# Two moves in a hand-written order: two weight products in front of a batch's scores, and softmax sums one group later

## The chip, the core and the metric

The kernel runs on one NeuronCore of a Trainium2 chip. The metric is the device time of one execution in microseconds (us). The inputs lie in device memory at the start, the output lies there at the end; the host does no arithmetic.

## What is computed

A Linformer attention over 8 batches of 8 heads, 1024 tokens, head size 64, followed by a feed-forward block with an activation close to hard-swish. Cut to what matters:

```python
k_proj = einsum('ks,bhsd->bhkd', E, k)          # 1024 tokens -> 64 rows
v_proj = einsum('ks,bhsd->bhkd', F, v)
attn   = softmax(q @ k_proj.T / 8)              # 1024 x 64 per head
x      = (attn @ v_proj).reshape(8 * 1024, 512)
h      = x @ w_in                               # 512 -> 2048
g      = h * clip(h + 3, 0, 6) / 6
out    = g @ w_out                              # 2048 -> 512
```

## The kernel before, in words

The work of a batch is done in two blocks of 512 tokens (`t` is 0 or 1), and a block has two halves.

The first half makes `g`. It is a row of 16 groups (`fo`, written L0 to L15 in the orders below): `first_group` multiplies 128 columns of `w_in` with the block's `xT` (8 matmuls, helper line L189), ACT takes the activation out of PSUM (L535), DVE multiplies and writes one chunk of `g` in bf16 (L536). PSUM has four buffers of the pool `mm` for this (`pmm`) and four of the pool `at` (`pat`).

The second half multiplies `g` with `w_out`. Except in the first block of all, it is done as seven block products in place of eight: `g` and `w_out` are cut into 2 x 2 blocks, and sums and differences of blocks are multiplied (class `Sums` makes those of `g`, POOL and an early part of the kernel those of `w_out`, in `w_sums`). A `Pair` covers two times 128 tokens; a block has a pair A and a pair B. A name such as A7 is product 7 of pair A: 16 matmuls of 128x256 (L189), in `step`. Which operands a product reads:

- 7: block a22 of `g` as it is, and a sum of weights. 2: a11 as it is, and a difference of weights. Both open a PSUM tile of their own and are copied out (L665); 5 accumulates into the tile of 2 and is copied out.
- 5: `sc` = a11 + a21 (`sums.c`). 6: a21, overwritten by a22 - a21 (`sums.a`). 1: `sb`, a difference of a11 and the new a21 (`sums.b`). 3: `sd` (`sums.d`, two pieces on POOL). 4: a12.
- 6, 1, 3 and 4 accumulate one after another into one tile, `self.x`; between them DVE subtracts what stands in it from a copy (`sub`, L136) and so gets the output rows. The next product may start only when that subtraction has read the tile.

A block's second half is done while the next block's first half runs. The order of all this on TensorE is written out by hand, engines run their own instructions in program order, and a framework adds the waits. Two orders matter here.

Batch 0's second block, lines 706 to 734. Its second half is not woven with groups, but with batch 1's attention, which comes in four visits (V0 to V3, `visit`, L278 for sums and values, L257 for scores). V0 computes the scores of heads in three pairs from `qT` and `kT`, which two transposing DMAs (L177) and one more (L240) have to bring, and the exps of them on ACT (L266): four score tiles in `pat`, two in `pmm`. V1 does the softmax sums of the first pair with a matmul over ones, its values, the scores of the fourth pair, logs (L195), the inverse (L201) and the exps of the fourth. V2 and V3 do the rest; R is the rest of a visit, the DVE products (L290) that write `xT` of batch 1. The four sums of blocks are made behind the steps that `added` names; `pair.copy` says which copies go to ACT (A7, B7, A5), the others go to DVE.

The blocks of batch 1 and later run through `START` (the first block of batch 1) and `ORDER`. Other work is hung on places of these orders by `at((t, place), work)`; `done(place)` runs it behind the place. From batch 2 on, the softmax sums are not matmuls: `add_up(j)` adds one pair's weights on DVE (L298, transposing), `sums_turned` and `spread_sums` (the reciprocal and two kinds of DMA, L319 and L325) bring their inverse back over all rows, and `some_values` multiplies with it. For batch 2 this is hung on batch 1's blocks (lines 767 to 776). `some_scores` gives the first pair's exps at once and lets those of the second be called one by one behind later groups (`pop`).

At the start of a block the first lines do `behind[0].sums.a(KH - 2, KH)` (the last two chunks of a21), then L0, then `sums.b` and `sums.d`, then the places hung on L0.

Of the kernel before, what the change touches and what calls it, by code (L numbers as in the profile page):

```python
# [15 lines left out]
def kernel(  # L16
# [11 lines left out]
    nc = tc.nc  # L28
# [45 lines left out]
    def g_tile():  # L74
        return gpool.tile([P, FO, TOK], bf16, tag="g", name="g")
# [52 lines left out]
    KH, MH = FO // 2, d_model // 2  # L128
# [76 lines left out]
    def behind_that(last, *what):  # L205
        mark = att.tile([1, 1], bf16, tag="mark", name="mark")
        nc.gpsimd.tensor_copy(mark, last)
        load_kqv(*what)
# [3 lines left out]
    class Attention:  # L212
# [38 lines left out]
        def scores(self, j, *allocs):  # L251
            qT = qT_dma[self.b]
            tiles = [alloc() for alloc in allocs]
            for a in range(2):
                for t in range(NB):
                    for r in range(2):
                        nc.tensor.matmul(tiles[r][t * KP:(t + 1) * KP, a * HT:(a + 1) * HT],  # L257
                                         self.kT[r * D:(r + 1) * D, 2 * j + a, :],
                                         qT[r * D:(r + 1) * D, j, a, t * HT:(t + 1) * HT],
                                         start=True, stop=True)  # L260
            return tiles
# [23 lines left out]
        def values(self, j, *allocs):  # L285
            return self.quads(lambda r, h: self.vp[r:r + KP, h, :], j, allocs)
# [7 lines left out]
        def add_up(self, *js):  # L294
            if self.parts is None:
                self.parts = att.tile([P, KO, 32], f32, tag="parts", name="parts", bufs=1)
            for j in js:
                nc.vector.tensor_reduce(out=self.parts[:, j], op=ALU.add, axis=mybir.AxisListType.X, apply_transpose=True,  # L298
                                        in_=self.aT[j].rearrange("p a r n -> p (a r n)").rearrange(
                                            "p (c i) -> p c i", i=32))  # L300
# [237 lines left out]
    def first_group(xT, t, g, fo):  # L538
        h_ps = pmm()
        h_part(h_ps, xT, t, fo, range(KO))  # L540
        h_out(h_ps, g, fo)
# [20 lines left out]
    def x_tile():  # L562
        return xpool.tile([P, KO, NB, TOK], bf16, tag="xT", name="xT")
# [45 lines left out]
    def pop():  # L609
        if later:  # L610
            later.pop(0)()
# [94 lines left out]
    sums = Sums(g[1])  # L706
    behind = [Pair(0, 1, sums, p, beside=pmm) for p in range(2)]
    TwoGroups(xT, 1, g[1]).parts((0, 1), (2, 3))
    for fo in range(2, FO):
# [6 lines left out]
            sub(b21, b21, b22, nc.gpsimd)  # L716
        elif fo == 5:
            second.projected()
    added = {"A7": lambda: sums.c(nc.vector), "A2": lambda: sums.a(0, KH), "A5": sums.b, "V1": sums.d}
    for what in "V0 A7 A2 B7 A5 V1 A6 R B2 A1 V2 B5 R A3 B6 V3 A4 B1 R".split():  # L720
        if what[0] == "V":
            while later:
                pop()
            rest = second.visit(int(what[1:]))
        elif what[0] == "R":
            rest()
        else:
            pair = behind["AB".index(what[0])]
            pair.copy = nc.scalar.copy if what in ("A7", "B7", "A5") else nc.vector.tensor_copy
            pair.step(int(what[1:]))  # L730
            pop()
        if what in added:
            added[what]()
# [10 lines left out]
    for b in range(1, B):  # L744
        if b + 1 < B:
            x_next = second.xT = x_tile()
        third = Attention(b + 2) if b + 2 < B else None

        plan = {}

        def at(place, *what):
            plan.setdefault(place, []).extend(what)

        def scores(*js):
            return lambda: second.some_scores(js)

        def values(*js):
            return lambda: second.some_values(*js)

        def add_up(*js):  # L760
            return lambda: second.add_up(*js)

        def spread(turned, inverted):
            at(turned, lambda: second.sums_turned())
            at(inverted, lambda: second.spread_sums())

        if b == 1:
            at((0, "L0"), second.projected)
            at((0, "L8"), second.load_next)
            at((0, "N5"), scores(0, 1))  # L770
            at((0, "L14"), add_up(0))
            at((0, "L15"), add_up(1))
            at((1, "L1"), scores(2, 3))
            at((1, "L2"), add_up(2))
            at((1, "L3"), add_up(3))
            spread((1, "B2"), (1, "L5"))
        elif b == 2:
            at((0, "L2"), second.projected)
            at((0, "A4"), second.load_next)
            at((0, "A4"), scores(0, 1))  # L780
            at((0, "B6"), scores(2))
            at((0, "L10"), add_up(0))
            at((0, "B1"), scores(3), add_up(1))
            at((0, "B3"), add_up(2))
            at((1, "A6"), add_up(3))
            spread((1, "A1"), (1, "L4"))
            at((1, "L4"), third.projected)
        elif b + 1 < B:
            if b == 3:
                at((0, "L1"), second.load_next)  # L790
            at((0, "L1"), scores(0, 1))
            at((0, "B7"), add_up(0))
            at((0, "A1"), scores(2, 3), add_up(1))
            at((0, "A3"), add_up(2))
            at((0, "A4"), add_up(3))
            spread((0, "B6"), (0, "L10"))
            if third:
                at((0, "B4"), lambda: third.projected(pause=False))
                if third.b + 1 < B:
                    at((1, "L12"), third.load_next)  # L800
        if b < 3:
            at((1, "N2"), values(0))
            at((1, "L12"), values(1))
            at((1, "B3"), values(2))
            at((1, "L14"), values(3))
            if b == 1:
                at((1, "B3"), lambda: behind_that(second.recs[1][:1, 0, :1], 3, "q"))
        elif b + 1 < B:
            at((1, "A1"), values(0, 1))
            at((1, "A4"), values(2, 3))  # L810

        def done(place):
            for f in plan.pop((t, place), ()):
                f()

        for t in range(NB):
            g = g_tile()
            sums = Sums(g)
            start = (b, t) == (1, 0)
            pairs = {"A": behind[0], "B": behind[1], "N": Pair(b, t, sums, 0, (b, t) == (B - 1, NB - 1))}  # L820
            if not start:
                behind[0].sums.a(KH - 2, KH)
            done("start")
            for what in START if start else ORDER:
                n = int(what[1:])
                if what[0] != "L":
                    pairs[what[0]].step(n)
                    done(what)
                    if what == ("N5" if start else "B3"):
                        sums.a(0, KH - 2)  # L830
                    continue
                if b < 4 and t == 0 and n < 2:
                    if n == 0:
                        first_two = TwoGroups(xT, t, g)
                    for fo in range(2):
                        first_two.part(fo, range(n * (KO - 1), KO - 1 + n))
                    if n == 1:
                        first_two.out()
                else:
                    first_group(xT, t, g, n)  # L840
                pop()
                if n == KH - 1:
                    sums.c()
                if not start and n == 0:
                    behind[0].sums.b()
                    behind[0].sums.d()
                done(what)
            behind = [pairs["N"], Pair(b, t, sums, 1, (b, t) == (B - 1, NB - 1))]
        assert not plan, plan
        second, xT = third, x_next  # L850

    sums = behind[0].sums
# [35 lines left out]
```

## Time and profile before

| what | us |
|---|---|
| three runs | 484.77, 486.40, 486.26; median 486.26 |
| the profiled execution | 484.99 |
| its span, first to last instruction | 483.2 |
| TensorE busy | 474.6 (98%) |
| DVE busy | 330.5 (68%) |
| ACT busy | 263.5 (55%) |
| GpSimd busy | 175.5 (36%) |

The profile has PE for TensorE's matmuls, PEld for its weight loads, DVE for VectorE, ACT for ScalarE, POOL for GpSimd and SP for SyncE, which issues DMAs. In the order of time a line has the start in us from the first instruction, the duration, the engine, the source line, what is written <- what is read, the shape, how many instructions are put together, and in brackets the idle time in front with what ended it. In the list of waits: who <- for what, total us, how often, the longest. Matmuls overlap, so a run of them is counted from start to start.

### The profile page before, as it was taken

How to read it: one execution, taken by the hardware profiler on the slowest of the kernel's cores; microseconds unless marked ns; L12 is line 12 of the kernel's file. 1: busy time of each engine (PE TensorE's matmuls, PEld its weight loads, DVE VectorE, ACT ScalarE, POOL GpSimd, SP SyncE). 2: the span in 40 equal slices, each digit the busy share in tenths (PEclk: the TensorE clock that was granted, in tenths of full speed). 3: DMA queues.
4: the chain of work that ended last, by engine and by line, in shares of the span. 5: the costliest groups of instructions: out<-in, count | busy, mean ns of one | idle time of the engine just before them, and what ended most of it. 6: DMA issues, size and time to landing. Idle time of an engine off the chain costs nothing.

```text
span 483.2 us, 14296 instructions
## 1 busy us (share of the span) xinstructions
PE 474.6 (98%) x6210; PEld 330.2 (68%) x6210; DVE 330.5 (68%) x546; ACT 263.5 (55%) x502; POOL 175.5 (36%) x107
## 2 busy tenths in 40 slices
PE   8899989999999999999999999999999999999997
PEld 3554558657676776776777777777777777777777
DVE  2582368678865858886777857777777977756463
ACT  3666588675457553745457454655547444445441
POOL 8634953134335231533423235330333333140420
PEclk9999999999999999999999999999999999999999
DMA  9999999864976979499998295955911081111012
GB/s 164 198 201 207 232 154 214 182 109 94 241 135 114 211 162 231 107 201 206 208 176 161 79 224 107 210 112 121 221 45 46 26 206 60 45 45 45 35 43 101
DMA packets 84590, 68.61 MB, mean 142 GB/s; under 512 B 38320, under 2 KB 70576, under 8 KB 84528
## 3 DMA queue, kind: packets, MB, share of 16 engines
q0 software_dynamic: 33008, 29.36, 39.0%
q1 hardware_dynamic: 51152, 37.83, 32.3%
q8 instruction: 48, 0.79, 0.7%
q10 hardware_dynamic: 368, 0.52, 0.4%
q14 instruction: 14, 0.11, 0.1%
HBM read 71.83 MB, written 16.97 MB: 184 GB/s over the span
## 4 chain that ended last, share of the span: by engine, by line
PE 93%; DMA 4%; POOL 1%; DVE 1%; SPq 0%; issue 0%; ACT 0%; POOLq 0%
PE mm L189 71%; PE at L189 18%; DMA w_in_sb<-in_moe_w_in_dram 2%; PE at L278 2%; PE at L257 2%; DMA qT<-q 1%; DMA k<-in_k_dram 1%; SPq L177 0%; PE at L447 0%; POOL q L103 0%; DVE g L536 0%; ACT r L535 0%; DVE parts L298 0%; POOL k L107 0%; PE at L427 0%
## 5 line engine op out<-in xcount | busy, mean ns | idle before, releaser
L189 PE MATMUL mm<-xT,w_in_sb 128*64 128x512 bf16 x2048 | 254.2, 380 | 0.3 <-DMA w_in_sb<-in_moe_w_in_dram 0.3
L536 DVE SCALAR_TENSOR_TENSOR g<-r,mm 128x512 bf16<-128x512 f32 x256 | 173.9, 683 | 114.4 <-ACT r L535 112.2
L535 ACT ACTIVATE r<-mm 128x512 f32<-128x512 f32 x256 | 152.1, 597 | 147.4 <-PE mm L189 130.5
L189 PEld LDWEIGHTS <-w_in_sb 128*64 128x64 bf16 x2048 | 114.3, 110 | 72.8 <-issue 6.5
L189 PEld LDWEIGHTS <-g 128*64 128x64 bf16 x2048 | 112.3, 110 | 30.4 <-issue 3.2
L136 POOL TENSOR_TENSOR sd<-g,sb 128x1024 bf16<-128x1024 bf16 x28 | 59.0, 2124 | 146.3 <-DVE sb L136 73.7
L133 POOL TENSOR_TENSOR sc<-g 128x2048 bf16<-128x2048 bf16 x14 | 57.0, 4069 | 111.7 <-DVE g L536 111.7
L189 PE MATMUL mm<-w_out_sb,g 128*64 128x256 bf16 (+1 forms) x1088 | 77.2, 286 | 0.0
L189 PE MATMUL at<-w_sums,g 128*64 128x256 bf16 x896 | 58.3, 273 | 0.7 <-DVE g L536 0.7
L665 ACT COPY m<-at 128x256 f32<-128x256 f32 x84 | 31.3, 373 | 24.8 <-PE at L189 24.7
L290 DVE TENSOR_TENSOR xT<-at,rec 128x512 bf16<-128x512 f32 x54 | 36.0, 683 | 1.6 <-DMA rec<-turned_rows 1.0
L189 PE MATMUL mm<-w_out_sb,sd 128*64 128x256 bf16 x480 | 31.1, 273 | 0.0
L189 PE MATMUL mm<-w_sums,sb 128*64 128x256 bf16 x480 | 31.0, 273 | 0.0
L189 PEld LDWEIGHTS <-sd 128*64 128x64 bf16 x480 | 26.7, 110 | 5.3
L189 PEld LDWEIGHTS <-sc 128*64 128x64 bf16 x480 | 26.4, 110 | 5.7 <-issue 0.8
L189 PEld LDWEIGHTS <-sb 128*64 128x64 bf16 x480 | 26.4, 110 | 5.3
L266 ACT ACTIVATE aT<-at 128x512 bf16<-128x512 f32 x52 | 29.2, 596 | 1.1 <-PE at L257 0.6
L298 DVE TRANSPOSE_TENSOR_REDUCE parts<-aT 128x32 f32<-128x1024 bf16 x24 | 29.7, 1237 | 0.0
L189 PE MATMUL at<-w_out_sb,sc 128*64 128x256 bf16 x448 | 29.3, 273 | 0.0
L136 DVE TENSOR_TENSOR o_sb<-m,mm 128x256 f32<-128x256 f32 x60 | 24.8, 413 | 3.6 <-PE mm L189 3.5
L136 DVE TENSOR_TENSOR g<-g 128x1536 bf16<-128x1536 bf16 (+2 forms) x29 | 20.4, 703 | 0.6
L136 DVE TENSOR_TENSOR sb<-g 128x2048 bf16<-128x2048 bf16 x15 | 18.3, 1220 | 0.1
(91 smaller groups left out, 275.6 us busy)
## 6 DMA issues: line engine op xcount, KB each, us to landing
out_dram<-o_sb SPq DMA_DIRECT2D x60, 256.0 KB, 4.1
rec<-turned_rows SPq DMA_DIRECT2D x48, 256.0 KB, 6.4
k<-in_k_dram POOLq DMA_DIRECT2D x7, 1024.0 KB, 10.2
v<-in_v_dram POOLq DMA_DIRECT2D x7, 1024.0 KB, 15.6
q<-in_q_dram POOLq DMA_DIRECT2D x7, 1024.0 KB, 20.6
w_out_sb<-in_moe_w_out_dram POOLq DMA_DIRECT2D x4, 512.0 KB, 14.8
w_in_sb<-in_moe_w_in_dram POOLq DMA_DIRECT2D x7, 256.0 KB, 10.0
k<-in_k_dram POOLq DMA_DIRECT2D x4, 256.0 KB, 5.7
```

The lines of the kernel that those rows point to most:

```text
L133: engine.tensor_tensor(out=out, in0=x, in1=y, op=ALU.add)
L136: engine.tensor_tensor(out=out, in0=x, in1=y, op=ALU.subtract)
L189: nc.tensor.matmul(ps[lo:lo + width], stationary[:, lo:lo + width], moving, **flags)
L257: nc.tensor.matmul(tiles[r][t * KP:(t + 1) * KP, a * HT:(a + 1) * HT], self.kT[r * D:(r + 1) * D, 2 * j + a, :], qT[r * D:(r + 1) * D, j, ...
L266: when(lambda r=r: nc.scalar.activation(aT[:, :, r, :], tiles[r].rearrange("p (a n) -> p a n", a=2), AF.Exp, scale=scale))
L278: nc.tensor.matmul(tiles[t][c:c + D], stationary(r, 2 * j + a), self.weights(j, a)[r:r + KP], start=True, stop=True)
L290: when(lambda t=t: nc.vector.tensor_mul(self.xT[:, j, t, :], av[t], rec[:, t]))
L298: nc.vector.tensor_reduce(out=self.parts[:, j], op=ALU.add, axis=mybir.AxisListType.X, apply_transpose=True, in_=self.aT[j].rearrange("p a ...
L535: nc.scalar.activation(r, h_ps, AF.Relu, bias=0.5, scale=1.0 / 6.0)
L536: nc.vector.scalar_tensor_tensor(g[:, fo, :], r, 1.0, h_ps, op0=ALU.min, op1=ALU.mult)
L665: self.copy(m, ps)
```

## The change

```diff
-    added = {"A7": lambda: sums.c(nc.vector), "A2": lambda: sums.a(0, KH), "A5": sums.b, "V1": sums.d}
-    for what in "V0 A7 A2 B7 A5 V1 A6 R B2 A1 V2 B5 R A3 B6 V3 A4 B1 R".split():
+    added = {"A7": lambda: sums.c(nc.vector), "V0": lambda: sums.a(0, KH), "A5": sums.b, "V1": sums.d}
+    for what in "A2 A7 V0 B7 A5 V1 A6 R B2 A1 V2 B5 R A3 B6 V3 A4 B1 R".split():
...
             at((0, "N5"), scores(0, 1))
-            at((0, "L14"), add_up(0))
-            at((0, "L15"), add_up(1))
+            at((0, "L15"), add_up(0))
+            at((1, "L0"), add_up(1))
             at((1, "L1"), scores(2, 3))
```

In batch 0's second block, products 2 and 7 of pair A are issued before V0, in this order; they stood behind it as 7, 2. So on ACT the copy of A7 stands in front of V0's six exps, on DVE the copy of A2 in front of `sc`, and the in-place difference `sums.a` is issued behind V0. The buffers of the pool `mm` go round otherwise: A2 and A7 take those of groups 12 and 13, the two score tiles of V0 those of 14 and 15, B7 the one that A7's copy frees, and V1's scores the two that V0's exps free.

In batch 1's first block, `add_up(0)` of batch 2 stands on DVE behind the last chunk of `g` (group 15), not in front of it, and `add_up(1)` stands behind group 0's chunk and `sb` of the next block; it stood behind group 15's chunk. The instructions of TensorE and ACT keep their order there. GpSimd's and SP's orders are the same in both kernels.

## The prediction

> **What bounds the kernel now.** I read the page first, then the list of waits, then the order of time around the two places that the diff touches.
>
> ```profile
> PE 474.6 (98%) x6210; PEld 330.2 (68%) x6210; DVE 330.5 (68%) x546; ACT 263.5 (55%) x502; POOL 175.5 (36%) x107
> ...
> PEclk9999999999999999999999999999999999999999
> ```
>
> TensorE is busy for 474.6 of 483.2 us, at full granted clock in every slice. So nothing can come from doing less: the change moves work and removes none. What it can win is TensorE idle time inside 60 to 130 us. The list of waits in that stretch shows what there is to win:
>
> ```profile
> PEld L257 <- DMA qT<-q: 2.0, 1, 2.0
> ...
> PE at L189 <- DVE g L536: 0.7, 1, 0.7
> ```
>
> Two stalls: about 2 us where scores wait for the transposed queries, 0.65 us where a product waits for the last piece of `g`. All else of TensorE's there is issue gaps of 0.2 to 0.4 us. Taken whole, the two would be some 2.5 us, or 0.5%, which is also about what a measurement of this kernel can tell from no change. The question is what is late next.
>
> **Part 1, products 2 and 7 of pair A ahead of V0.** These lines are the order of time around V0:
>
> ```profile
> 58.56 8.80 PE L189 MATMUL mm<-xT,w_in_sb 128*64 128x512 bf16 x80
> ...
> 67.29 0.63 PE L257 MATMUL at<-qT,kT 64*64 64x256 bf16 x16
> ...
> 67.90 2.06 ACT L266 ACTIVATE aT<-at 128x512 bf16<-128x512 f32 x4
> 68.03 0.69 DVE L536 SCALAR_TENSOR_TENSOR g<-r,mm 128x512 bf16<-128x512 f32 x1 [0.18 <-ACT r L535]
> ...
> 69.62 0.41 PE L257 MATMUL mm<-qT,kT 64*64 64x256 bf16 x8 [1.70 <-DMA qT<-q]
> ...
> 69.96 2.81 PE L189 MATMUL mm<-w_sums,g 128*64 128x256 bf16 x48
> ...
> 71.07 0.37 ACT L665 COPY m<-mm 128x256 f32<-128x256 f32 x1
> ...
> 73.69 0.37 ACT L665 COPY m<-mm 128x256 f32<-128x256 f32 x1 [0.50 <-PE mm L189]
> ...
> 74.02 1.08 ACT L195 ACTIVATE rec<-at 128x512 f32<-128x512 f32 x2
> ...
> 75.14 1.06 ACT L201 ACTIVATE rec<-rec 128x1024 f32<-128x1024 f32 x1
> ...
> 76.23 1.29 DVE L290 TENSOR_TENSOR xT<-at,rec 128x512 bf16<-128x512 f32 x2 [0.29 <-ACT rec L201]
> ...
> 77.55 0.51 PE L278 MATMUL at<-aT,ones 64*64 64x512 bf16 x4
> ```
>
> The reader is to see three things. TensorE idles from 67.66 to 69.62 before the eight scores of the third pair of heads. ACT has one exp after another from 67.90. And the sums of 77.55 start just when the DVE products (76.23 + 1.29 = 77.52) let go of their PSUM tiles.
>
> TensorE's side. The 80 matmuls from 58.56 take 0.108 each, so TensorE is free at 67.2. A product is 16 matmuls; the 48 from 69.96 end where the next group begins, at 72.61, so one is 0.87. A2 runs 67.2 to 68.1, A7 to 68.95. A2 reads chunks of `g` that are long written, and its PSUM buffer was freed at 66.1. A7's last two matmuls come at 68.84 and need the chunk that DVE writes from 68.03 to 68.72: no wait. V0's first 16 scores then run from 69.05 to 69.4, and the last eight still wait for the second transpose, which lands at 69.58 whatever TensorE does. So V0 ends at 69.96 as now, but B7 comes next, instead of A7 and A2: TensorE is **1.73 us ahead** here (2 x 0.87).
>
> ACT's side. The copy of A7 now stands in front of the six exps, not behind them. It can start 0.25 after A7, at 69.2, and holds ACT for 0.33 (73.69 to 74.02). The exps, which started at 67.90, start at 69.53. They start 0.49 apart, so ACT gets to the copies of B7 and A5 at 72.45, 0.33 each, and to V1's two logs at 73.12. Now those start at 74.02. So ACT is only **0.90 ahead** of now. Two waits of TensorE take the rest: V1's scores need two PSUM buffers that the last two exps read until 72.57 (TensorE comes at 72.25: 0.35), and V2's sums need the tiles that the DVE products read. These follow the logs: 1.12 to the inverse, 1.06 for it, 1.29 for two products. That was 77.52 and becomes 76.62, so B5 starts at 77.08 and not 77.98.
>
> From 77.54 to 83.84 ACT stands still for nothing (its rows of logs and inverses follow each other), and the chain of logs, inverses and products feeds the next hidden layer; so 0.90 stays, neither more nor less. DVE: A2's copy now comes before `sc`, which ends at 70.20 instead of 69.86, needed by A5 at 70.83. The in-place difference and `sb` come at 70.23 and 71.48 instead of 72.28 and 73.53. sd on GpSimd follows `sb` and ends at 77.0; A3 needs its second half at 78.4. The orders of GpSimd and SP are the same, and loads and transposes of batch 2 are triggered by the same transposes. The k and v of batch 2 land 9.7 and 13.9 us after issue, v at 81.1, and are used at 83.7: cover of 2.6. Its q lands at 86.9; its transposes are due at 88.1: cover of 1.2, and behind that 2 us more until the scores. Value taken: -0.90. Bounds: 0, if the logs start where they do now; -1.73, if neither wait comes.
>
> **Part 2, sums over batch 2's weights one group later.** I keep the present clock; part 1 shifts all of it alike.
>
> ```profile
> 103.88 1.24 DVE L298 TRANSPOSE_TENSOR_REDUCE parts<-aT 128x32 f32<-128x1024 bf16 x1
> ...
> 104.17 0.93 PE L189 MATMUL at<-w_sums,g 128*64 128x256 bf16 x14
> ...
> 105.04 0.65 DVE L536 SCALAR_TENSOR_TENSOR g<-r,mm 128x512 bf16<-128x512 f32 x1
> ...
> 105.75 0.30 PE L189 MATMUL at<-w_sums,g 128*64 128x256 bf16 x2 [0.65 <-DVE g L536]
> ...
> 110.00 0.69 DVE L536 SCALAR_TENSOR_TENSOR g<-r,mm 128x512 bf16<-128x512 f32 x1 [0.19 <-ACT r L535]
> ...
> 117.31 0.35 DVE L136 TENSOR_TENSOR o_sb<-mm,m 128x256 f32<-128x256 f32 x1
> ...
> 117.84 1.04 PE L189 MATMUL mm<-w_out_sb,g 128*64 128x256 bf16 x16
> ```
>
> DVE has the sum of 103.88 in front of the last gated piece of `g` (105.04), and the last two matmuls of A7 wait for this until 105.75. With the sum behind it, the piece starts when ACT gives its input, 104.25, and ends at 104.94, when TensorE arrives at 104.93. TensorE leaves A7 at 105.09, not 105.88: **0.79 ahead**.
>
> But DVE does the same work, and it is what is full: from 103.28 to 117.97 its rows follow each other with one gap, 0.19 at 110.00. I add start to start. Now, 103.28 to 110.00: 6.72. After: gated piece 0.97 (0.37 of it idle until 104.25), piece 0.60, sum 1.16, in-place difference 0.30, piece 0.60, `sb` 1.13, sum 1.16, piece 0.60, subtraction 0.31: 6.83. So DVE is 0.11 later from there, the 0.19 gap used up. Behind it TensorE waits: A1, A3 and A4 accumulate into the PSUM tile that DVE's subtractions read. A1 comes at 110.10 and may start at 110.26; A3 comes at 113.73, may start at 114.06; A4 comes at 117.53 and may start when the subtraction of 117.31 is done, now 0.11 later, at 117.77 plus 0.04. It starts at 117.84 today. The 0.79 turns into three waits of 0.16, 0.33 and 0.28, and **0.03** remains. The reciprocal is 0.1 later, so the spread sums too; the products with them wait for that transfer already (1.02 at 124.73) and TensorE needs the first at 126.2, 0.7 after it. Bounds: -0.79, if DVE made room; +0.12, if the gap of 0.19 is not recovered either (0.30 later, less 0.18 of slack in front of A4).
>
> **Sum.** -0.90 - 0.03 = -0.93. The profiled execution took 484.99 (span 483.2 and 1.8 around it): 484.1. The three runs have 484.77, 486.26 and 486.4, so the median lies 1.3 above the profiled one, and from the median it is 485.3. The four times spread over 1.6 us; I take the value between the two sums, **484.7**.
>
> A rule against the change: the Trainium skill, "SBUF — State Buffer", section "SBUF: two separate sides", says that a transfer issued from GpSimd cannot write its descriptors while VectorE holds the port the two share. Here GpSimd issues q at 70.77, when DVE had ended `sc` at 69.86 and was idle until 71.94. After the change three DVE operations stand back to back from 68.98 to 72.71. By the rule the issue would slip to 72.8 at worst, q would land at 88.9 and sd would end near 78; both still have cover, so the sum would be the same.
>
> **Rivals.**
> (a) Both stalls are won whole: -1.73 - 0.79 = -2.5, 482.5 from the profiled time and 483.8 from the median. For it: the stalls are real. Against it: the ACT chain and DVE's full rows. 0.08.
> (b) Nothing arrives. ACT's order costs more than counted (each copy in front of the exps moves all behind it), or part 2 loses its 0.12: within 0.4 of now, 484.8 to 486.4. 0.20.
> (c) Slower. GpSimd's issue of q and, queued behind it, sd starve beside DVE's three back-to-back operations, and go on only after DVE's next full stretch, the products that end at 76.62. The issue then ends at 77.5 and sd at 81.8; A3 needs its second half at 78.4: 3.4 lost, 2.5 slower in all, 487.5 to 488.7. It decides from an issue that starts after 75.0, where the loss passes 0.9. Against it: issues of k and v at 66.27 and 67.18 took 0.91 and 0.88 beside DVE's gated pieces, q's 0.89 beside an idle DVE. 0.04.
> The forecast: 0.68. Range: 483.0 to 486.5, from most of (a) to all of (b). Chances: faster by over 0.5% only in half of (a) and by scatter, 0.06; slower 0.04; within, 0.90.
>
> **What would show it.** Right: no wait for `qT` over 0.3 us; A7's copy on ACT before the exps, these back to back, logs 0.9 ahead of now; TensorE waiting for ACT at V1 and near V2; no 0.65 wait for `g`, and in its place waits of A1, A3 and A4 for DVE. Wrong: V2's sums 1.7 ahead (a); logs where they are (b); sd late in front of A3 (c).

## The result and the profile after

After: 484.59 us median of 22 runs (483.62 to 485.48). Before, run beside it: 485.25 of 22 (484.57 to 487.0). The ratio is 0.9978 with a 95% interval of 0.9968 to 0.9987: faster by about 0.2%, inside the 0.5% that were called no change. The medians alone differ by 0.14%; the ratio also takes in the longer executions of before that are told of at the end ("Open"). The forecast was 484.7. The profiled execution of after took 483.99, against 484.99 of before.

The page of after, its first lines:

```profile
span 482.2 us, 14296 instructions
...
PE 474.7 (98%) x6210; PEld 330.6 (69%) x6210; DVE 330.5 (69%) x546; ACT 263.3 (55%) x502; POOL 175.6 (36%) x107
```

The busy times are those of before within 0.4 us, and the span is 1.0 shorter: work was moved, none taken away. That 1.0 isn't yet the change's effect. I compared the two traces at ACT's activations of the hidden layer (L535), which come in the same order in every kernel here, and wrote down how much earlier or later each starts:

| place (us in before) | after against before | step |
|---|---|---|
| 22.7, first loads, untouched by the diff | -0.48 | -0.48 |
| 87.6, first hidden layer of batch 1 | -1.51 | **-1.03**, part 1 |
| 107.0, behind A7 | -2.27 | **-0.76**, part 2's stall |
| 119.9, behind A4 | -1.53 | **+0.74**, three waits |
| 135.5 | -0.99 | **+0.54**, near 133 |
| end | -1.00 | 0 |

The first 0.48 comes from the arrival of the first loads. It lies between -0.9 and +0.16 in the thirteen profiles of this study, whatever was changed, so each profile is read from the last place in front of part 1 on (67.4, where after still stands at -0.48; e1_again and e9_recip_early come 0.04 and 0.09 later between 35 and 50 us, which belongs to no part). To put a time of after into before's clock, add 0.48 up to 77 us and 1.5 in part 2's stretch (part 2's own steps left in).

Around V0, in order of time (after):

```profile
66.72 1.91 PE L189 MATMUL mm<-w_sums,g 128*64 128x256 bf16 x32
...
68.67 0.38 ACT L665 COPY m<-mm 128x256 f32<-128x256 f32 x1 [1.15 <-PE mm L189]
69.02 2.06 ACT L266 ACTIVATE aT<-at 128x512 bf16<-128x512 f32 x4
69.02 0.40 PE L257 MATMUL mm<-qT,kT 64*64 64x256 bf16 x8
...
69.35 1.06 PE L189 MATMUL mm<-w_sums,g 128*64 128x256 bf16 x16
...
70.16 0.89 POOL L121 DMA_DIRECT2D q<-in_q_dram  x1 [2.61 <-issue]
...
71.90 0.70 ACT L665 COPY m<-mm 128x256 f32<-128x256 f32 x2
72.11 0.41 PE L257 MATMUL mm<-qT,kT 64*64 64x256 bf16 x7 [0.17 <-ACT aT L266]
...
72.41 1.18 ACT L195 ACTIVATE rec<-at 128x512 f32<-128x512 f32 x2
...
73.63 1.06 ACT L201 ACTIVATE rec<-rec 128x1024 f32<-128x1024 f32 x1
...
74.72 1.29 DVE L290 TENSOR_TENSOR xT<-at,rec 128x512 bf16<-128x512 f32 x2 [0.69 <-ACT rec L201]
...
76.47 0.58 PEld L189 LDWEIGHTS <-sc 128*64 128x64 bf16 x12 [0.31 <-issue]
```

The third pair's scores (69.02) wait for no transpose. The copy of A7 (68.67) stands in front of the exps on ACT, the copies of B7 and A5 (71.90) behind them, and the logs at 72.41, which is 72.89 in before's clock. B7 starts at 69.35, and B5, the product over `sc`, at 76.47, or 76.95. Before, B5 stood here:

```profile
77.98 1.06 PE L189 MATMUL mm<-w_out_sb,sc 128*64 128x256 bf16 x16
```

Around A7, A1, A3 and A4 of batch 1's first block (after):

```profile
102.65 1.13 PE L189 MATMUL at<-w_sums,g 128*64 128x256 bf16 x16
102.74 0.69 DVE L536 SCALAR_TENSOR_TENSOR g<-r,mm 128x512 bf16<-128x512 f32 x1 [0.29 <-ACT r L535]
103.34 1.24 DVE L298 TRANSPOSE_TENSOR_REDUCE parts<-aT 128x32 f32<-128x1024 bf16 x1
...
108.27 0.41 DVE L136 TENSOR_TENSOR o_sb<-m,mm 128x256 f32<-128x256 f32 x1
...
108.73 1.06 PE L189 MATMUL mm<-w_sums,sb 128*64 128x256 bf16 x16
...
112.07 0.38 DVE L136 TENSOR_TENSOR o_sb<-m,mm 128x256 f32<-128x256 f32 x1
...
112.51 1.06 PE L189 MATMUL mm<-w_out_sb,sd 128*64 128x256 bf16 x16
...
115.89 0.35 DVE L136 TENSOR_TENSOR o_sb<-mm,m 128x256 f32<-128x256 f32 x1
...
116.29 1.06 PE L189 MATMUL mm<-w_out_sb,g 128*64 128x256 bf16 x16
```

A7 (102.65) runs its 16 matmuls in one row; before, the last two stood apart behind a wait of 0.65. But A1, A3 and A4 (108.73, 112.51, 116.29) each start 0.05 to 0.06 after the end of the subtraction in front of them (108.68, 112.45, 116.24). TensorE now waits for DVE in three places in place of one.

The stretch behind, where the spread sums come back (after; SPq is SyncE issuing):

```profile
115.02 0.94 DVE L316 RECIPROCAL inv<-inv 64x128 f32<-64x128 f32 x1
...
115.99 0.81 SPq L319 DMA_DIRECT2D turned_rows<-inv  x2
...
118.50 5.19 SPq L325 DMA_DIRECT2D rec<-turned_rows  x8
...
123.64 1.29 DVE L290 TENSOR_TENSOR xT<-at,rec 128x512 bf16<-128x512 f32 x2 [1.47 <-DMA rec<-turned_rows]
...
127.15 1.29 DVE L290 TENSOR_TENSOR xT<-at,rec 128x512 bf16<-128x512 f32 x2 [0.70 <-DMA rec<-turned_rows]
...
133.14 0.68 DVE L536 SCALAR_TENSOR_TENSOR g<-r,mm 128x512 bf16<-128x512 f32 x1
...
133.88 0.11 PEld L189 LDWEIGHTS <-g 128*64 128x64 bf16 x2 [0.46 <-DVE g L536]
```

Before, the same products, and the next product 7 without a wait:

```profile
124.73 1.29 DVE L290 TENSOR_TENSOR xT<-at,rec 128x512 bf16<-128x512 f32 x2 [1.02 <-DMA rec<-turned_rows]
...
127.56 1.28 DVE L290 TENSOR_TENSOR xT<-at,rec 128x512 bf16<-128x512 f32 x2
...
134.00 1.16 PE L189 MATMUL at<-w_sums,g 128*64 128x256 bf16 x16
```

The products waited once, 1.02 at 124.73, and those at 127.56 not at all. Now both pairs wait. In before's clock the second starts at 128.7, 1.1 later, and what stands behind it on DVE is later too, up to the chunk of `g` at 133.14 that the last two matmuls of the next product 7 need.

### The profile page after: what moved, and what is told of

Read it like the earlier page. It is cut to its first block, busy times and chain, and to the rows that moved or that the text cites. A ratio compares the mean times of both kernels' runs of the same rounds, so it can differ in the third digit from the quotient of the medians.

```text
span 482.2 us, 14296 instructions
## 1 busy us (share of the span) xinstructions
PE 474.7 (98%) x6210; PEld 330.6 (69%) x6210; DVE 330.5 (69%) x546; ACT 263.3 (55%) x502; POOL 175.6 (36%) x107
## 4 chain that ended last, share of the span: by engine, by line
PE 87%; DMA 4%; DVE 3%; ACT 2%; POOL 2%; issue 1%; SPq 1%; POOLq 0%
PE mm L189 67%; PE at L189 17%; DMA v<-in_v_dram 2%; DMA rec<-turned_rows 2%; PE at L257 1%; PE at L278 1%; DVE g L536 1%; DVE parts L298 1%; ACT aT L266 1%; SPq L325 1%; POOL q L103 1%; POOL k L107 1%; POOL v L107 0%; DMA turned_rows<-inv 0%; DVE xT L290 0%
## 5 line engine op out<-in xcount | busy, mean ns | idle before, releaser
L535 ACT ACTIVATE r<-mm 128x512 f32<-128x512 f32 x256 | 152.1, 598 | 147.4 <-PE mm L189 129.6
## 6 DMA issues: line engine op xcount, KB each, us to landing
v<-in_v_dram POOLq DMA_DIRECT2D x7, 1024.0 KB, 15.6
```

The costliest lines, as they stand in the source:

```text
L535: nc.scalar.activation(r, h_ps, AF.Relu, bias=0.5, scale=1.0 / 6.0)
```

## The experiments

The theory after the result: part 1's gain is what ACT's queue lets through; part 2's gain is given back because DVE is full up to A4; and part 2 costs half a microsecond more, because the spread sums land late. The rivals: TensorE's own order sets part 1's gain, and its nearness to the forecast is chance; the give-back near 133 is scatter, or comes from part 1; the three waits stand there for another reason than DVE's load.

Times carry the ratio to before, run beside each, with its interval. Steps are read as in the table above. Executions of one kernel differ by half a microsecond and more, so the steps are what tells theories apart, and the times confirm them.

**The change again, and each part alone.** The first has no edit. Part 1 alone (e2_part1) is before with:

```diff
-    for what in "V0 A7 A2 B7 A5 ...
+    for what in "A2 A7 V0 B7 A5 ...
```

and `sums.a` behind V0; part 2 alone (e3_part2) is before with the two `add_up` lines of the diff.

> The changed kernel once more, on the chip of the next three. In its first profile TensorE gained 1.03 us at V2 and 0.03 by A4 of the next block, and lost 0.54 again near 133 us, where the last two matmuls of a product 7 waited for DVE, whose products had waited 1.47 and 0.70 for the spread sums (0.56 later than before, from store to issue of the spread). Theory: the gain to A4 is the same here to 0.1; the loss near 133 is set by when the spread sums land and varies from execution to execution, 0 to 0.6. Rival: the loss belongs to the new order and stands at 0.5 again. Time against the kernel before: 0.6 to 1.6 less.

> Products 2 and 7 in front of V0, the softmax sums where they were. Theory (part 1 carries all, the ACT queue sets it): B5 starts 1.0 us ahead of before, the wait of product 7 for the last chunk of g near 105 stays at 0.65, and the time is that of the changed kernel within 0.2. Rival (part 2 carries some of it): the time lies 0.4 to 0.8 above the changed kernel's.

> The softmax sums one group later, the products behind V0 as they were. Theory (DVE is full from 103 to 118 us): the wait of 0.65 goes, A7 ends 0.75 ahead, three new waits in front of A1, A3 and A4 take it back, A4 starts within 0.1 of where it does before; the time is that of the kernel before within 0.3. Rival (the gain of 0.75 stays): 0.75 less than before.

| run | time, ratio | part 1 | A7 | to A4 | near 133 |
|---|---|---|---|---|---|
| e1_again | 484.47, 0.9987 (0.9978 to 0.9995) | -1.04 | -0.75 | +0.73 | -0.01 |
| e2_part1 | 483.97, 0.998 (0.997 to 0.9989) | -1.04 | 0 | 0 | -0.12 |
| e3_part2 | 486.27, 1.0027 (1.0016 to 1.0039) | -0.13 | -0.75 | +0.73 | +0.61 |

Part 1 brings the same 1.03 to 1.04 in every profile that has it in this form. Part 2 wins its stall and gives it back to 0.02, with or without part 1. The time of part 1 alone was expected within 0.2 of the changed kernel's and lies 0.50 below e1_again's. Part 2 alone was expected within 0.3 of before and is slower, by 1.2 us in the medians; its profile accounts for about 0.5 of them from 22.7 on, and the rest stays open. The loss near 133 is there with part 2 and not in e2_part1; in e1_again it is missing too, and that is taken up below.

**Is ACT's queue what holds part 1?** e4_split takes the third pair's scores out of V0, and does A2 and A7 behind the first two pairs, so that the exps start before the copy of A7 and still no scores wait at the head of TensorE's order. e7_copies leaves the order and takes the copies of B7 and A5 off ACT.

```diff
-    for what in "A2 A7 V0 B7 A5 ...
+    for what in "V0 A2 A7 V4 B7 A5 ...        # e4_split; V4: scores and exps of the third pair
...
-            pair.copy = nc.scalar.copy if what in ("A7", "B7", "A5") else nc.vector.tensor_copy
+            pair.copy = nc.scalar.copy if what == "A7" else nc.vector.tensor_copy   # e7_copies
```

> The changed kernel with V0 cut in two: the scores of the first two pairs in front of A2 and A7, those of the third pair behind them. ACT gets its first exps 1.6 us sooner, TensorE does the same work in the same time up to B7. Theory (in the changed kernel the ACT queue, begun late, takes 0.7 of TensorE's 1.73): TensorE waits nowhere up to V2, B5 starts 1.7 ahead of the kernel before, 0.7 ahead of the changed one, and the time is 0.5 to 0.8 below the changed kernel's. Rival (something else holds V2, such as DVE or PSUM buffers): the time is the changed kernel's within 0.2.

> The changed kernel with the copies of B7 and A5 on DVE in place of ACT. They held ACT for 0.51 between the exps and V1's logs; DVE is idle from 72.2 to 73.6 there. Theory (the ACT queue sets V2): the logs start 0.5 sooner and B5 0.4 to 0.5 sooner, and the time falls by 0.3 to 0.5 against the changed kernel. Rival (PSUM buffers or DVE set it): no gain, within 0.2, or a loss since A1 gets sb later.

e4_split, in order of time:

```profile
67.46 2.06 ACT L266 ACTIVATE aT<-at 128x512 bf16<-128x512 f32 x4
...
69.84 1.06 PE L189 MATMUL mm<-w_sums,g 128*64 128x256 bf16 x16
...
71.81 0.37 ACT L668 COPY m<-mm 128x256 f32<-128x256 f32 x1 [0.50 <-PE mm L189]
...
72.15 1.08 ACT L195 ACTIVATE rec<-at 128x512 f32<-128x512 f32 x2
...
76.11 1.06 PE L189 MATMUL mm<-w_out_sb,sc 128*64 128x256 bf16 x16
```

e7_copies, in order of time:

```profile
69.45 1.06 PE L189 MATMUL mm<-w_sums,g 128*64 128x256 bf16 x16
...
71.77 1.09 ACT L195 ACTIVATE rec<-at 128x512 f32<-128x512 f32 x2
...
75.74 1.06 PE L189 MATMUL mm<-w_out_sb,sc 128*64 128x256 bf16 x16
...
77.36 0.36 PEld L189 LDWEIGHTS <-sd 128*64 128x64 bf16 x8 [0.39 <-POOL sd L136]
```

In e4_split the exps start 1.6 earlier than in after (67.46 against 69.02), with heads only 0.04 apart, and B5 comes at 76.11: 1.43 ahead of before. In e7_copies (head -0.68) B5 comes at 75.74, or 76.42 in before's clock: 1.56 ahead, nearly TensorE's whole 1.73. There A3 then waits 0.39 for sd on POOL, since `sb` now stands behind the two copies on DVE, and 1.26 remain at the first hidden layer. Nothing in TensorE's list of products was changed in e7_copies. From B7 to B5 TensorE takes 6.25 in before (71.73 to 77.98), 7.12 in after, and 6.27 and 6.29 in these two. In e2_part1, with the same order, B7 starts 0.32 later than in after, both in before's clock, and B5 still comes at the same 76.95. So what after loses there, some 0.85, was ACT's queue and not TensorE's own order; in e4_split ACT now waits for TensorE (0.50 at 71.81). With ACT's limit gone the next one stands close behind, sd on POOL. The 1.7 at B5 and the 0.5 to 0.8 in time that were expected of e4_split did not come: the missing 0.3 lies in front of B7, where the third pair's scores still wait 0.2 for the second transpose. The times, 484.35 (0.9981, 0.9972 to 0.9991) and 484.26 (0.9981, 0.9971 to 0.9992), can't be told from after's, because both kernels keep part 2 and lose 0.79 and 0.45 near 133.

**Are the three waits of A1, A3 and A4 DVE's load?** Two of the four sums of batch 2 (`add_up(2)` and `add_up(3)`, 1.24 each) are left out, with POOL writing a constant in their place. e5_room_old has the first two sums in their old places, e6_room_new in the new ones; both have part 1.

```diff
-            at((1, "L2"), add_up(2))
-            at((1, "L3"), add_up(3))
+            at((1, "L2"), lambda: nc.gpsimd.memset(second.parts[:, 2], 1.0))
+            at((1, "L3"), lambda: nc.gpsimd.memset(second.parts[:, 3], 1.0))
```

> Products 2 and 7 in front of V0, the softmax sums in their old places, but those of batch 2's third and fourth pair left out (GpSimd sets these sums to one, so that batch 2's output is scaled wrongly). It is the base for the next kernel: DVE has 2.4 us less to do between 110 and 114 us. The wait of 0.65 for the last chunk of g stays, since it comes before that. The spread sums land some 2 us sooner, so the products near 124 do not wait. Time: 0 to 0.5 below products 2 and 7 in front of V0 alone.

> The changed kernel with the same two sums left out (batch 2's output is scaled wrongly). Theory (moving the first two sums gains 0.75 at A7, and only DVE's full queue takes it back): with the queue relieved from 109 us on, the waits of A3 and A4 go, that of A1 (0.1 to 0.2) stays, and A4 starts 0.6 sooner than in the kernel with the old places and the same sums left out; the time is 0.5 to 0.7 below it. Rival (the gain at A7 is lost whatever DVE has to do): the same time within 0.2.

e6_room_new, in order of time:

```profile
108.19 0.41 DVE L136 TENSOR_TENSOR o_sb<-m,mm 128x256 f32<-128x256 f32 x1
...
108.65 1.06 PE L189 MATMUL mm<-w_sums,sb 128*64 128x256 bf16 x16
...
109.99 0.41 DVE L136 TENSOR_TENSOR o_sb<-m,mm 128x256 f32<-128x256 f32 x1
...
112.12 1.07 PE L189 MATMUL mm<-w_out_sb,sd 128*64 128x256 bf16 x16
```

A1 (108.65) still starts right behind its subtraction, which the sums left out don't touch. A3's subtraction now ends at 110.4, and A3 starts at 112.12 without waiting for it. Of the 0.75 won at A7 0.63 stay, and only A1's 0.12 goes back. e5_room_old has nothing to win or lose there: 0. The times are 483.72 (0.9969, 0.9958 to 0.998) and 482.94 (0.9961, 0.9948 to 0.9973). So the theory holds: part 2's stall was real, and DVE's full rows took it back.

**Is the loss near 133 the landing of the spread sums?** The reciprocal and its store hang on group 5 (`spread`'s second place). e8_recs_later puts them one group later, e9_recip_early behind B2, where the sums of the last pair are turned.

```diff
-            spread((1, "B2"), (1, "L5"))
+            spread((1, "B2"), (1, "L6"))          # e8_recs_later
+            spread((1, "B2"), (1, "B2"))          # e9_recip_early
```

> The changed kernel with the reciprocal of batch 2's sums and the transfers behind it one group later (place L6, not L5), so that the spread sums land 1.3 to 2 us later. Theory (the loss near 133 us comes from the landing of the spread sums, through DVE's queue, and there is no slack left): the wait of the product 7 near 133 grows and the time rises by 1 to 2 us against the changed kernel. Rival (DVE catches up before 133): the same time within 0.3.

> The changed kernel with the reciprocal of batch 2's sums directly behind their transposing (place B2, not L5): the stores of the inverse go out 0.6 us sooner. In four of five profiles with the later sums, the second of these stores left 0.09 later than before, nine of its 144 packets stood behind a transfer of kind instruction of 8 KB, it landed 0.6 to 0.8 later than before, and the product 7 near 133 us waited 0.45 to 0.8. Theory (that collision makes the loss): the store is through before the instruction transfer, the second issue of the spread follows the end of the reciprocal by 2.0 and not 2.5 to 2.7, the loss near 133 goes, the time falls by 0.3 to 0.6 against the changed kernel. Rival (the loss comes from DVE's later queue, whatever the store does): the loss of about 0.5 near 133 stays.

e9_recip_early, in order of time:

```profile
114.09 0.94 DVE L316 RECIPROCAL inv<-inv 64x128 f32<-64x128 f32 x1
...
117.03 5.18 SPq L325 DMA_DIRECT2D rec<-turned_rows  x8
...
122.55 1.29 DVE L290 TENSOR_TENSOR xT<-at,rec 128x512 bf16<-128x512 f32 x2 [0.71 <-DMA rec<-turned_rows]
...
125.70 1.28 DVE L290 TENSOR_TENSOR xT<-at,rec 128x512 bf16<-128x512 f32 x2
```

The first products wait 0.71 in place of 1.47, the second not at all, and the loss near 133 is gone (-0.12 instead of +0.54): 483.31 us, 0.9962 (0.9949 to 0.9974), an interval that does not overlap e1_again's and just overlaps after's (from 0.9968 on). e8_recs_later goes the other way, as it should if the landing is the cause; its order of time:

```profile
116.23 0.94 DVE L316 RECIPROCAL inv<-inv 64x128 f32<-64x128 f32 x1
...
128.66 1.29 DVE L290 TENSOR_TENSOR xT<-at,rec 128x512 bf16<-128x512 f32 x2 [1.02 <-DMA rec<-turned_rows]
...
133.59 0.84 PE L189 MATMUL mm<-xT,w_in_sb 128*64 128x512 bf16 x6 [0.68 <-DVE g L536]
```

Its profile loses 0.91 by 128 and 1.13 more near 133, for a reciprocal 1.2 later. The loss in the times is smaller than the 1 to 2 that were expected: 484.72, 0.9995 (0.9985 to 1.0005), which is 0.13 and 0.25 above the medians of after and e1_again, with intervals that overlap. So it is the profile that shows it.

But part 2 makes the reciprocal only 0.1 later, and the loss is 0.54. The list of SP's waits shows where the rest comes from. It has one line for the wait of the second DMA (L325) for the first (L319). After:

```profile
SPq L325 <- DMA turned_rows<-inv: 1.6, 1, 1.6
```

e9_recip_early:

```profile
SPq L325 <- DMA turned_rows<-inv: 1.1, 1, 1.1
```

It is 1.6 to 1.8 in the five profiles that have part 2 with the reciprocal on group 5 (after, e1, e3, e4, e7), and 1.1 in before and in the eight others. The two DMAs of L319 are 144 small packets each. In after the transfers from 117.4 on, queue by queue, first up to 117.6:

```profile
q1 hardware_dynamic: 70, 0.01, 25.6%
```

and from 117.6 to 117.8:

```profile
q1 hardware_dynamic: 9, 0.00, 3.5%
```

So 9 of the 144 packets, a sixteenth, come last. Between 117.0 and 117.4 one transfer of 8 KB of the kind "instruction" (queue q14) starts, and the nine packets start when it ends, to 0.01 us, in each of the five profiles with the long wait. The landing of the second DMA is signalled in sixteen parts: in these five the last signal comes 0.46 to 0.73 behind the fifteenth (118.44 against 117.90 in after), in the nine others 0.01 to 0.02. Counted from group 0's activation, the second half of the store starts 0.09 later than in before (14.23 against 14.15), and the instructions 0.3 earlier (14.2 to 14.3 in all nine profiles with part 2, 14.6 in the five without): in before they come behind the store's last packet. In e8_recs_later they come in front of its first (117.4 to 117.6, the packets 118 to 119). So a sixteenth of the store was late behind the instructions. That this sixteenth belongs to one of the 16 DMA engines, and that this one was busy with the instructions, is inferred: the trace doesn't name the engine of a packet. Why the instructions come earlier wasn't tried, and neither was the meeting by itself: e9_recip_early avoids it and has the reciprocal 0.6 earlier as well.

What stays open here: e1_again has the long wait of SP (1.6) and lost nothing, because its second piece of `rec` happened to land sooner; and e11_split_p1_v below has the short wait (1.1) and lost 0.34, with a second piece that landed late. So the landing also scatters by some tenths from one execution to the next, and one profile per kernel doesn't give the mean.

**What both lessons together bring.** e10_split_p1 is e4's order without part 2. e11_split_p1_v adds to it the projection of batch 4 (`third.projected`) one group later, because its `v` landed late in some profiles. e12_split_all has e4's order, part 2, e9's early reciprocal and that later projection.

```diff
-            at((1, "L4"), third.projected)
+            at((1, "L5"), third.projected)        # e11_split_p1_v, e12_split_all
```

> V0 cut in two and products 2 and 7 between the parts, the softmax sums where they were in the kernel before. Theory (the later sums bring nothing up to A4 and cost near 133; V0 cut in two brings 0.4 more than products 2 and 7 in front of the whole V0): TensorE is 1.4 ahead of before at the first hidden layer, loses nothing near 133, and the time is 0.2 to 0.5 below that of part 1 alone, 1.3 to 1.6 below before. Rival (what is gained early is given back at the next landing): the time of part 1 alone within 0.2.

> The same with the projection of batch 4 one group later (place L5, not L4). In four of ten profiles so far TensorE waited 0.25 to 0.44 near 169 us for v of batch 4: it is read 15.8 after its issue and lands 15.6 to 16.2 after it. Theory (that is one source of the scatter): no gap at that place, and the median is 0.1 to 0.3 below the same kernel without it, with less scatter. Rival (the landing follows the place it is read, or the chain to the scores gets late): no gain, or 0.3 to 1 more near 190.

> V0 cut in two, the softmax sums later, the reciprocal early, the projection of batch 4 one group later: both parts of the change, each with what took its gain taken away. Theory: 1.4 ahead at the first hidden layer, 0 more up to A4 (DVE is still full there), nothing lost near 133 and 169: the time of the kernel above within 0.2. Rival (later sums still cost): 0.3 to 0.6 more than the kernel above.

| run | time, ratio | part 1 | A7 to A4 | near 133 | near 170 |
|---|---|---|---|---|---|
| e10_split_p1 | 483.52, 0.9962 (0.9948 to 0.9976) | -1.44 | 0 | +0.07 | 0 |
| e11_split_p1_v | 483.70, 0.9962 (0.9949 to 0.9974) | -1.44 | 0 | +0.34 | 0 |
| e12_split_all | 483.31, 0.9956 (0.9943 to 0.9968) | -1.43 | -0.02 | -0.12 | 0 |

e12_split_all has the lowest ratio of all complete kernels here, 0.44% below before; its interval ends where after's begins (0.9968), and it can't be told from e9, e10 and e11. In the medians of five runs e10 came out 1.8 below before where 1.3 to 1.6 were expected, and e12 0.39 below e11 where 0.2 was the most. Part 2 adds nothing to e12 up to A4: what it has beyond e10 in the profiles lies near 133 (0.19), no more than the landing scatters. The later projection hides a late `v`: it took 16.1 and 16.2 us to land in e11 and e12, as late as in the profiles that lost 0.25 to 0.44 near 170, and nothing was lost. In the times that doesn't show (483.70 against 483.52 for e10), so what it is worth stays unsettled.

## Why the prediction was right

**What bounds the kernel.** Right: busy times the same, gain only from TensorE's idle time, and less than the two stalls' 2.5.

**Part 1, -0.90.** Measured -1.03, by the mechanism named: no wait for `qT`, A7's copy ahead of the exps, logs earlier, B5 behind the DVE products. The size was 0.13 off. The copies of B7 and A5 were taken at 0.33 each, 0.66 in all; from the start of the first to the logs they took 0.51 (71.90 to 72.41), and the first started 0.07 sooner than reckoned (72.38 in before's clock, not 72.45). The way from the logs to the inverse, 1.22 (72.41 to 73.63) and not 1.12, gave 0.10 of that back. TensorE's 1.73 did not arrive; e4_split and e7_copies show that ACT's queue kept it back, and that 1.43 to 1.56 could be had by B5.

**Part 2 up to A4, -0.03.** Measured -0.02, out of -0.76 at A7 (predicted -0.79) and steps back of 0.13, 0.30 and 0.31 (predicted 0.16, 0.33, 0.28). e6_room_new shows DVE's load as the cause.

**The step that failed** is the last one of part 2: "The reciprocal is 0.1 later, so the spread sums too; the products with them wait for that transfer already (1.02 at 124.73) and TensorE needs the first at 126.2, 0.7 after it." Two things in it were wrong. In the five profiles the second transfer of the sums (L325) was issued 0.6 to 0.8 later and not 0.1, with a sixteenth of the store late behind the instructions. And the slack was looked up at the wrong reader: not TensorE's use of the first pair's values ends it, but DVE's queue. The second products wait in it, with the chunks of `g` behind them, and TensorE waits for one of these at 133.88. The bound of +0.12 for part 2 was too narrow by that: +0.52 in the profile.

**The sum.** -0.93 against a span 1.00 shorter looks exact, and isn't: -0.48 of the first loads, -1.03, -0.02 and +0.54. In the medians the change brings 0.66 where part 1 alone brings 1.08 (e2_part1), so part 2 costs some 0.4 to 0.5 there as well (e1_again against e2_part1: 0.50). That the forecast of 484.7 came within 0.1 was luck of the same kind: it amounts to 0.93 below 485.6, a base between the runs known then, and that base proved 0.4 above the 485.25 of 22 runs while the gain was 0.3 too large.

**The rivals.** (a) fell at ACT and DVE, as argued. (b) has a part of the truth: part 2 did lose, and by more than 0.12, only in a place that neither it nor the forecast looked at. (c) did not come: POOL's issue of q took 0.89 at 70.16, 70.64 in before's clock against 70.77, although DVE ran `sc`, the in-place difference and `sb` from 68.49 to 72.23 without a gap. The prediction had applied the rule of the Trainium skill, "SBUF — State Buffer", section "SBUF: two separate sides", to any VectorE operation, which would put the issue at about 72.2. The section is narrower: it names copies, casts and `tensor_scalar` as able to take the shared port pair in a two-port mode, and says that `tensor_tensor` was not seen to stall a DMA. All three operations here are TENSOR_TENSOR in the profile, so the 0.89 agrees with the section as it stands.

**Open.** Why part 2 alone is slower by more than its profile shows. Nine of before's 22 runs lie at 486.26 to 487.0 and none of after's above 485.5; no profile was taken of such a run. The runs beside the experiments have their granted TensorE clock on record: it was 0.996 in 10 of 69 executions without part 1 (8 of 62 of before, with a median of 486.48 against 485.06 for the other 54, and 2 of 7 of e3_part2), and never under 0.999 in 110 with part 1, those of after among them. So most of the long runs go with a lower clock, seen only in kernels where TensorE still waits some 2 us for `qT`, and part 1 may bring more in the times than the profiles show. Whether that wait lowers the clock wasn't tested. How often the store meets the instruction transfer in executions without a profile wasn't measured.

## What to carry to other kernels

When a stall of TensorE goes, follow each engine's queue behind the moved instructions up to the next thing that TensorE takes from it: here ACT's order set one gain (1.03 of 1.73) and DVE's load took the other back (0.74 of 0.76). An instruction that already waits for a transfer has no slack: count what stands behind it in its queue, and where a chain of small DMAs hangs on it, start that chain as early as its data allow, as the reciprocal one place earlier did (in the profiles 0.54 lost became 0.12 won). Check a sum that comes out right by its terms, from a place ahead of the change on: the end of the span alone would have called this one exact.

## What the runs showed of the hardware

- A transfer of instructions can hold up a small store: one of 8 KB went with a wait for 2 x 144 packets of 1.6 to 1.8 us in place of 1.1, and with one of the store's sixteen landing signals 0.46 to 0.73 behind the others; shifts of 0.1 and 0.3 us brought the two together.
- The arrival of the first loads moves all that follows by up to 1.1 us between executions (-0.9 to +0.16 against before).
- The landing of a 1 MB load scatters, and the wait for it can go by another name. `v` of batch 4 was read 15.8 us after its issue in every kernel with the projection on group 4; in after it landed after 15.6 and nothing waited. In e1_again, by the view of the tile `v`:

```profile
DMA to landing us min/median/max: 16.2/16.2/16.2
```

It was issued at 152.6, so it landed at 168.8. There, in order of time, TensorE goes on behind an idle time that the profile calls "issue", not DMA:

```profile
168.83 0.11 PEld L189 LDWEIGHTS <-e_t 128*64 128x64 bf16 x1 [0.55 <-issue]
```

That cost e1_again 0.43 near 170. With the projection on group 4, the five profiles whose `v` took 16.0 to 16.2 lost 0.25 to 0.44 there, and the seven with 15.5 to 15.8 at most 0.03; on group 5 (e11, e12) 16.1 and 16.2 cost nothing.
- Three TENSOR_TENSOR operations of DVE on bf16 tiles, back to back for 3.7 us, did not slow an issue of POOL beside them (0.89 us, as with DVE idle).
